# The q projection of two chunks as one Strassen pair, moved behind wo of the first chunk

## The chip, the cores and the metric

The kernel runs on one core of one Trainium2 chip. The metric is the device time of one execution in microseconds (us), lower is better. A core has a matrix engine (TensorE), a vector engine (VectorE), a scalar engine (ScalarE), GpSimd, and SyncE, which only issues transfers. Each engine works through its own instructions in order and waits on semaphores for the others. Sixteen DMA engines move data between device memory and the on-chip memory. In the profile the engines are called PE, DVE, ACT, POOL and SP.

## The reference, cut to what matters

One transformer layer on 2048 tokens of width 1024: layer norm, q, k and v of 32 heads of 32, attention of each position to itself and seven earlier ones at a stride of two, the output projection wo, a residual, then a second norm and a gated feed-forward part (FFN).

```python
qkv = (x @ wqkv) -> q, k, v                       # 32 heads of 32
idx = pos[:, None] - arange(8)[None, :] * 2        # 8 positions each
logits = einsum("bhsd,bhswd->bhsw", q, k[idx]) * 32 ** -0.5
o = einsum("bhsw,bhswd->bhsd", softmax(logits), v[idx])
h = x + o @ wo
g, u = layernorm(h) @ w_gate, layernorm(h) @ w_up
return h + (g * u) @ w_down
```

Inputs and outputs are bfloat16.

## The kernel before

The tokens are split into four chunks of 512. TensorE makes q, k and v of a chunk in 24 groups of 8 matmuls (6 weight blocks of 4 groups: blocks 0 and 1 are q, 2 and 3 are k, 4 and 5 are v). ScalarE copies each group out of PSUM (the memory into which TensorE writes; this kernel uses it as eight banks of 512 columns), SyncE stores it to device memory, GpSimd loads the whole of a chunk back in another layout for VectorE. VectorE does the attention. Its output takes the same way: one store of 1 MB (`od`), four reloads of a quarter each (`oT`), and then wo on TensorE.

```python
def attention(c):                                  # VectorE, about 84 us a chunk
    ...                                            # 4 x products q * k, sums: lg
    nc.scalar.activation(lg[:], lg[:], ACTF.Exp, scale=float(DH) ** -0.5)
    ...                                            # sums, 1/sum, 4 x products with v: oD
    nc.gpsimd.dma_start(od[c].rearrange("c g d s -> (c g) d s"), oD[:])
    oT = att.tile([128, KO, 4, SUB], BF, tag="oT", name=f"oT{c}")
    for cp in range(4):
        nc.gpsimd.dma_start(oT[:, :, cp, :], od[c][cp].rearrange("(hg hl) d s -> (hl d) hg s", hl=4))
    ...

def abs_down():                                    # ScalarE: sums of |w_down| for a later stage
    ring = wpool.tile([128, KO, 512], BF, tag="w", name="w_ring")
    ...
    for p in range(2):
        load(p)                                    # a load that ScalarE issues itself
    yield "later", 12.0
    for p in range(7):
        scale_d.add(p, rows_of(p), rows_of(p))
        ...
```

A generator such as `attention` or `abs_down` is background work. After each group of TensorE a scheduler, which runs when the kernel is built, takes the next steps of it. So the order within VectorE and ScalarE is fixed at build time, by a model of time.

The main order, cut:

```python
qkv(0, range(1, 4))
load_qk(0)                                         # q and k of chunk 0 back, for attention 0
...
bg.add(norm1[3].sums(), bg.now + 18.0)             # norm of chunk 3 on ScalarE
start_attention(0)
sums = abs_down()
bg.add(sums, bg.now + 25.0, first=True)
qkv(1, range(4))
qkv(0, range(4, 6))
load_v(0)
bg.add(norm1[3].rows(), bg.now, first=True)
qkv(1, range(4, 6))
start_attention(1)
...
qkv(2, range(6))
...
qkv(3, range(4), last=True)                        # q and k of chunk 3; frees weights
bg.finish(atts[0])
...
nxt = wo_ln2(0)                                    # wo of chunk 0 and its norm on VectorE
qkv(3, range(4, 6), last=True)                     # v of chunk 3: fills TensorE meanwhile
...                                                # then the FFN of chunk 0
```

Of the kernel before, what the change touches and what calls it, by code (L numbers as in the profile page):

```python
# [18 lines left out]
D = 1024  # L19
# [59 lines left out]
def kernel(  # L79
# [45 lines left out]
    bg = Background()  # L125

# [132 lines left out]
    class NormOnScalar(Norm1):  # L259
# [16 lines left out]
        def devs(self):  # L276
            nc.scalar.activation(self.nm, self.s, ACTF.Copy, scale=-1.0 / D)
            for t in range(4):
                nc.scalar.activation(self.junk[:], self.xs[t][:], ACTF.Square, bias=self.nm[:, t:t + 1],
                                     accum_out=self.ss[:, t:t + 1])  # L280
                yield "later", self.pace
            nc.scalar.activation(self.rs4[:], self.ss, ACTF.Ln, bias=eps[:], scale=1.0 / D)
# [17 lines left out]
        def rows(self):  # L300
            for t in range(4):
                self.row(t)
                self.transpose(t)
                yield "later", self.pace

# [33 lines left out]

    qkv_in = {}  # L340

    def evac_qkv(c, m, ps):
        sg = t1k.tile([128, HB + TC], BF, tag="t1k", name=f"sg{c}_{m}")
        nc.scalar.copy(sg[:, HB:HB + TC], ps[:])  # L344
# [5 lines left out]
        if m < 8:  # L350
            nc.sync.dma_start(qd[c][:, 4 * hg:4 * hg + 4, :, :].rearrange("c g d s -> (g d) c s"),
                              sg[:, HB:HB + TC].rearrange("p (c s) -> p c s", c=4))
# [81 lines left out]
    def qkv(c, blocks, last=False):  # L434
        for b in blocks:
            for j in range(4):
                ps = psum.tile([128, TC], F32, tag="mm", name=f"ps{c}_{b}_{j}")
                mm_group(ps, wts["qkv", b], j, lnTs[c])
# [9 lines left out]
    def load_qk(c):  # L448
        qD = att.tile([128, DH, SUB], BF, tag="qD", name=f"qD{c}")
        kD = att.tile([128, DH, SUB + HB], BF, tag="kD", name=f"kD{c}")  # L450
        nc.gpsimd.dma_start(qD[:], qd[c].rearrange("c g d s -> (c g) d s"))
# [98 lines left out]
    class Norm2(NormOnScalar):  # L550
# [11 lines left out]
        def finish(self):  # L562
            yield from self.devs()
# [5 lines left out]
    def wo_norm(c):  # L569
# [4 lines left out]
        for t in range(4):  # L574
            for hf in range(2):
# [6 lines left out]
                if hf == 0 and t > 0:  # L582
                    n.sum(t - 1)
                bg.step(GROUP_US)
        n.sum(3)
        retire(2)
        return n

    def wo_ln2(c, at={}):
        lnT = lnTp.tile([128, KO, TC], BF, tag="lnT", name=f"lnT2_{c}")  # L590
        hs = hss[c]
        mv4, rs4 = ln_tiles(f"2_{c}")

        def norm(t):
            ln = normalize(hs[t], mv4, rs4, t)
            nc.sync.dma_start_transpose(lnT[:, :, bass.ts(t, 128)], ln[:])

        for t in range(4):
            for hf in range(2):
                ps = psum.tile([128, 512], F32, tag="mm", name=f"wo{c}_{hf}_{t}")  # L600
                for kk in range(KO):
                    nc.tensor.matmul(ps[:], lhsT=oTs[c][:, kk, t, :], rhs=wts["wo", c, hf][:, kk, :],
                                     start=(kk == 0), stop=(kk == KO - 1))
                nc.vector.tensor_tensor(hs[t][:, bass.ts(hf, 512)], ps[:], hs[t][:, bass.ts(hf, 512)], ALU.add)
                if hf == 1:
                    stats(hs[t], mv4, t)
                    rstd_of(mv4, rs4, t, t + 1)
                    bg.spend(1.5)
                elif t > 0:
                    norm(t - 1)  # L610
                    bg.spend(0.55)
                bg.spend(0.7)
                if 2 * t + hf in at:
                    at[2 * t + hf]()
                bg.step(GROUP_US)
        norm(3)
        retire(2)
        for t in range(4):
            rows = hsd[c][:, t, :]
            nc.sync.dma_start(rows, hs[t][:, D - rows.shape[-1]:D])  # L620
        return lnT, hs



    ones = const.tile([128, 128], BF)
    nc.vector.memset(ones[:], 1.0)

    class Scale:
        def __init__(self, name, n):
# [724 lines left out]
```

## Time and profile before

| | before |
|---|---|
| time, median of the first 3 runs | 771.18 us (770.24 to 771.34) |
| profiled span, mean granted TensorE clock | 768.7 us, 1.000 |
| TensorE busy | 99% |
| VectorE busy | 79% |
| wo of chunk 0 starts | 163.45 us |
| FFN starts | 191.07 us |

TensorE is busy nearly all of the time and has almost no waits, so the span is close to the number of 512-column matmuls times 0.216 us plus the start. The prediction below shows the lines for that. Three more views matter for what follows. First the timeline of GpSimd (start, length, engine, line, operation, tiles, count, and in brackets the idle time before it and what ended it), with the k load of attention 0 (`kD`) and the store of its output (`od`):

```profile
44.12 0.54 POOL L452 DMA_DIRECT2D kD<-kd  x1 [12.56 <-DMA kd<-sg]
...
136.85 0.54 POOL L536 DMA_DIRECT2D od<-oD  x1 [47.11 <-DVE oD L534]
```

Second the transfers issued between 125 and 165 us (tiles, issuing queue, count, size of each, and the median time from issue to landing in us):

```profile
od<-oD POOLq DMA_DIRECT2D x1, 1024.0 KB, 4.2
```

The store of 1 MB took 4.2 us. It was not quite alone: SyncE issued four loads of 256 KB from 138.10 us on. But both wo weight loads (1 MB each) were issued after it had landed, from 145.50 us on. Third the timeline of ScalarE where it issues the first two loads of the down weights:

```profile
66.72 1.16 ACTq L671 DMA_DIRECT2D w_ring<-in_B_w_down_dram  x2
```

That held ScalarE's queue for 1.16 us.

### The profile page before, as it was taken

The page shows a single profiled execution, that of the slowest core. Times are in us where ns is not written, and L with a number is a line of the kernel's source. Part 1 is how long each engine was busy: PE and PEld are TensorE (multiplying, and loading weights), DVE is VectorE, ACT ScalarE, POOL GpSimd, SP SyncE. Part 2 cuts the span into 40 slices and gives each one's busy share as a digit, 9 for nine tenths or more (in the row PEclk, how much of TensorE's full clock was granted, in tenths as well). Part 3 has the DMA queues.
Part 4 walks back from the last instruction along what each step waited for, and adds up shares of the span by engine and source line. Part 5 has one row for each costly group of instructions (what it writes and reads, how often), then busy time and mean ns, then how long its engine had stood idle before and what let it go on. Part 6 is the DMA issues. An engine that isn't in the chain of part 4 may idle for free.

```text
span 768.7 us, 10302 instructions
## 1 busy us (share of the span) xinstructions
PE 762.8 (99%) x3663; PEld 350.7 (46%) x3663; DVE 606.0 (79%) x718; ACT 513.1 (67%) x979; POOL 142.5 (19%) x152
## 2 busy tenths in 40 slices
PE   8999999999999999999999999999999999999998
PEld 5444444444444444444444444444444444444444
DVE  5639999999999999999998997975454444568863
ACT  4648966423687398778899986736777677788240
POOL 0000000200002000020000001018778677600000
PEclk9999999999999999999999999999999999999999
DMA  8999796999966699579559448674342423730001
GB/s 268 272 257 260 207 269 153 279 305 283 301 219 216 210 299 294 172 246 326 194 186 300 139 155 279 126 198 107 80 110 55 110 74 91 257 126 29 0 29 55
DMA packets 190915, 144.85 MB, mean 188 GB/s; under 512 B 81808, under 2 KB 181136, under 8 KB 188688
## 3 DMA queue, kind: packets, MB, share of 16 engines
q1 hardware_dynamic: 180416, 116.94, 54.2%
q0 software_dynamic: 3584, 22.02, 8.4%
q10 hardware_dynamic: 6864, 5.24, 2.5%
q8 instruction: 28, 0.46, 0.2%
q14 instruction: 23, 0.19, 0.1%
HBM read 110.10 MB, written 27.26 MB: 179 GB/s over the span
## 4 chain that ended last, share of the span: by engine, by line
PE 97%; DVE 2%; DMA 1%; issue 0%; ACTq 0%; DVEq 0%
PE ps L431 21%; PE dx L944 6%; PE pz L826 6%; PE pwu L431 6%; PE pu L431 6%; PE py L826 6%; PE pwg L431 6%; PE pg L431 6%; PE px L826 6%; PE wo L998 4%; PE pv L826 3%; PE ez L944 3%; PE ey L944 3%; PE ex L944 3%; PE dy L944 3%; PE wo L578 2%
## 5 line engine op out<-in xcount | busy, mean ns | idle before, releaser
L431 PE MATMUL ps<-lnT,w_qkv 128*128 128x512 bf16 x736 | 159.5, 379 | 0.0
L431 PEld LDWEIGHTS <-w_qkv 128*128 128x128 bf16 x736 | 71.9, 98 | 86.1 <-issue 0.2
L344 ACT CAST sg<-ps 128x512 bf16<-128x512 f32 x96 | 55.2, 586 | 46.9 <-PE ps L431 41.6
L477 DVE TENSOR_TENSOR prod<-qD,kD 128x4096 bf16<-128x4096 bf16 x32 | 72.2, 2284 | 12.8 <-DMA kD<-kd 12.8
L523 DVE TENSOR_TENSOR pv<-vD,at 128x4096 bf16<-128x4096 bf16 x32 | 72.4, 2285 | 0.2
L826 PEld LDWEIGHTS <-sw 128*128 128x128 f16 x448 | 43.8, 98 | 52.9 <-issue 0.2
L431 PEld LDWEIGHTS <-w_wu 128*128 128x128 bf16 x448 | 43.8, 98 | 52.9
L431 PEld LDWEIGHTS <-w_wg 128*128 128x128 bf16 x448 | 43.8, 98 | 52.9
L826 PE MATMUL px<-lnT,ws 128*128 128x512 bf16 x224 | 55.2, 379 | 0.0
L536 POOL DMA_DIRECT2D od<-oD x4 | 2.2, 544 | 275.6 <-DVE oD L534 275.6
L431 PE MATMUL pg<-lnT,w_wg 128*128 128x512 bf16 x224 | 52.9, 379 | 0.0
L431 PE MATMUL pu<-lnT,w_wu 128*128 128x512 bf16 x224 | 52.9, 379 | 0.0
L431 PE MATMUL pwu<-lnT,w_wu 128*128 128x512 bf16 x224 | 52.9, 379 | 0.0
L431 PE MATMUL pwg<-lnT,w_wg 128*128 128x512 bf16 x224 | 52.9, 379 | 0.0
L826 PEld LDWEIGHTS <-ws 128*128 128x128 f16 x336 | 32.9, 98 | 39.6
L807 POOL TENSOR_TENSOR sw<-ws 128x512 f16<-128x512 f16 x26 | 30.0, 1155 | 82.4 <-PE pv L826 49.1
L944 PEld LDWEIGHTS <-gs 128*128 128x128 f16 (+1 forms) x280 | 27.4, 98 | 33.0
L479 DVE TENSOR_TENSOR prod<-prod 128x4096 bf16<-128x4096 bf16 x16 | 36.6, 2288 | 0.4
L843 ACT COPY py<-px 128x512 f32<-128x512 f32 x28 | 16.0, 570 | 27.7 <-PE px L826 27.7
L808 POOL TENSOR_TENSOR sw<-sw,ws 128x512 f16<-128x512 f16 x26 | 30.0, 1154 | 2.0
L810 POOL TENSOR_TENSOR sw<-ws,sw 128x512 f16<-128x512 f16 x26 | 30.3, 1167 | 0.0
L809 POOL TENSOR_TENSOR sw<-ws 128x512 f16<-128x512 f16 x26 | 30.1, 1156 | 0.0
(334 smaller groups left out, 1472.9 us busy)
## 6 DMA issues: line engine op xcount, KB each, us to landing
w_wg<-in_B_w_gate_dram SPq DMA_DIRECT2D x14, 1024.0 KB, 6.9
w_wu<-in_B_w_up_dram SPq DMA_DIRECT2D x14, 1024.0 KB, 6.3
w_pair<-in_B_w_gate_dram SPq DMA_DIRECT2D x14, 512.0 KB, 4.0
w_pair<-in_B_w_up_dram SPq DMA_DIRECT2D x14, 512.0 KB, 5.3
w_wo<-in_A_wo_dram SPq DMA_DIRECT2D x6, 1024.0 KB, 7.6
w_qkv<-in_A_wqkv_dram SPq DMA_DIRECT2D x5, 1024.0 KB, 11.5
kd<-sg SPq DMA_DIRECT2D x32, 144.0 KB, 4.4
kD<-kd POOLq DMA_DIRECT2D x4, 1152.0 KB, 8.6
```

The lines of the kernel that those rows point to most:

```text
L344: nc.scalar.copy(sg[:, HB:HB + TC], ps[:])
L431: nc.tensor.matmul(ps[:], lhsT=wt[:, ko, bass.ts(j, 128)], rhs=rhs[:, ko, :], start=(ko == 0), stop=(ko == KO - 1))
L477: nc.vector.tensor_tensor(prod[:, j], qD[:], kD[:, :, o:o + SUB], ALU.mult)
L479: nc.vector.tensor_tensor(prod[:, :, 0:16], prod[:, :, 0:16], prod[:, :, 16:32], ALU.add)
L523: nc.vector.tensor_tensor(pv[:, j], vD[:, :, o:o + SUB], at[:, w, None, :].to_broadcast((128, DH, SUB)), ALU.mult)
L807: eng.tensor_tensor(sw[:, i, 0], a21, a22, ALU.add)
L808: eng.tensor_tensor(sw[:, i, 1], sw[:, i, 0], a11, ALU.subtract)
L809: eng.tensor_tensor(sw[:, i, 2], a11, a21, ALU.subtract)
L810: eng.tensor_tensor(sw[:, i, 3], a12, sw[:, i, 1], ALU.subtract)
L826: nc.tensor.matmul(ps[:], lhsT=lhs[:, ko, :], rhs=rhs[:, ko, :], start=(fresh and ko == 0), stop=(ko == 3), skip_group_check=not fresh)
L944: nc.tensor.matmul(ps[:, bass.ds(lo, n)], lhsT=lhs[k][:, bass.ts(q, 128)], rhs=rhs[k][:, bass.ds(lo, n)], start=(fresh and k == 0), stop=( ...
L998: nc.tensor.matmul(ps[:], lhsT=oTs[c][:, kk, t, :], rhs=wts["wo", 2, hf][:, kk, :], start=(kk == 0), stop=(kk == KO - 1))
```

## The change

Strassen's scheme computes a 2 x 2 block product with 7 block products instead of 8. The change applies it to q of chunks 2 and 3 together (the two column blocks are the two chunks), with the halves of the contraction as the other dimension. It needs sums and differences of weight blocks and of activation rows in float16, so the q weights are first scaled by a power of two, which comes from the sum of their absolute values. That saves 16 matmuls. The pair also serves as filler: it stands behind wo of chunk 0, where TensorE computed v of chunk 3 before. Alongside, the first q load waits until chunk 1's transposes have landed, the norm of chunk 0 moves from VectorE to ScalarE, and the background work of ScalarE starts a little earlier.

The diff, cut to its core:

```diff
+    def add(self, k, src, junk):                  # class Scale, only moved up
+        nc.scalar.activation(junk, src, ACTF.Abs, accum_out=self.l1[:, k:k + 1])
 ...
-    def load_qk(c):
+    def load_qk(c, after=None):
 ...
+        if after is not None:
+            nc.gpsimd.tensor_copy(qD[:, 0, 0:1], after)
 ...
-    qkv(0, range(1, 4))
-    load_qk(0)
+    qkv(0, [1], at={(1, k): (lambda k=k: q_abs(k)) for k in range(4)})
+    qkv(0, [2], at={(2, 2): scale_q.rows})
+    qkv(0, [3], at={(3, 2): scale_q.total, (3, 3): q_convert})
+    load_qk(0, after=lnTs[1][:, 0, TC - 1:TC])
+    start_attention(0)
+    qkv(1, [2])
 ...
-    bg.add(norm1[3].sums(), bg.now + 18.0)
+    bg.add(norm1[3].both(), bg.now + 16.0, first=True)
     sums = abs_down()
-    bg.add(sums, bg.now + 25.0, first=True)
-    qkv(1, range(4))
+    bg.add(sums, bg.now + 18.0, first=True)
+    qkv(1, [3, 0, 1])
 ...
-    qkv(2, range(6))
+    qkv(2, range(2, 6))
 ...
-    qkv(3, range(4), last=True)
+    qkv(3, range(2, 6), last=True)
     bg.finish(atts[0])
 ...
-    nxt = wo_ln2(0)
-    qkv(3, range(4, 6), last=True)
+    rows_q = q_row_sums()                         # 12 + 1 sums of activation rows, VectorE
+    bg.add(rows_q, bg.now, first=True)
+    norm2 = [wo_norm(0, devs=False)]
+    bg.finish(rows_q)
 ...
+    for m0 in (0, 2):
+        q_pair(m0, room_q)                        # 112 matmuls instead of 128
```

## The prediction

> **What bounds the kernel now.** I began with the page: busy shares, the 40 slices, the chain that ended last.
>
> ```profile
> span 768.7 us, 10302 instructions
> PE 762.8 (99%) x3663; PEld 350.7 (46%) x3663; DVE 606.0 (79%) x718; ACT 513.1 (67%) x979; POOL 142.5 (19%) x152
> PE   8999999999999999999999999999999999999998
> DVE  5639999999999999999998997975454444568863
> PE 97%; DVE 2%; DMA 1%; issue 0%; ACTq 0%; DVEq 0%
> ```
>
> TensorE is busy from about 17 us to the end and is 97% of the chain, so removing matmuls pays directly. But VectorE has next to no air between slices 4 and 22 (about 77 to 420 us). A shorter TensorE stretch there pays only as far as VectorE's results are there in time. So I read next the timeline of TensorE where the change acts (columns: start, length, engine, line, operation, tiles, count).
>
> ```profile
> 27.04 136.57 PE L431 MATMUL ps<-lnT,w_qkv 128*128 128x512 bf16 x632
> 163.45 13.98 PE L602 MATMUL wo<-w_wo,oT 128*128 128x512 bf16 x64
> 177.26 13.98 PE L431 MATMUL ps<-lnT,w_qkv 128*128 128x512 bf16 x64
> 191.07 1.89 PE L431 MATMUL pg<-lnT,w_wg 128*128 128x512 bf16 x8
> 253.23 13.98 PE L578 MATMUL wo<-w_wo,oT 128*128 128x512 bf16 x64
> ```
>
> No idle time stands in any of these lines. 64 matmuls take 177.26 - 163.45 = 13.81 us, which is 0.216 us each, and a group of 8 takes 1.727 us. (The 379 ns that the groups view gives for one is latency.) Then VectorE, and GpSimd's issues, for the two attention chunks whose outputs TensorE needs at 163.45 and at 253.23:
>
> ```profile
> 52.34 4.49 DVE L477 TENSOR_TENSOR prod<-qD,kD 128x4096 bf16<-128x4096 bf16 x2 [12.77 <-DMA kD<-kd]
> 134.26 2.29 DVE L534 TENSOR_TENSOR oD<-oD,pv 128x4096 bf16<-128x4096 bf16 x1
> 172.30 1.28 DVE L604 TENSOR_TENSOR h<-wo,h 128x512 bf16<-128x512 f32 x2
> 141.35 3.55 POOL L539 DMA_DIRECT2D oT<-od x4 [3.96 <-DMA od<-oD]
> 244.34 3.54 POOL L539 DMA_DIRECT2D oT<-od x4 [6.39 <-DMA od<-oD]
> ```
>
> Attention 0 waits for its k load until 52.34, then runs without a gap of note to 136.55. Its output passes through memory: the first quarter of oT was issued at 141.35 and took 6.6 us to land, so it is there at 147.95, 15.5 us before use. For chunk 1 it lands at 244.34 + 3.7 = 248.05, 5.2 us before use. The first addition of wo in VectorE (172.30) is some 7 us behind TensorE's first finished group (163.45 + 1.9): VectorE is still in attention 1, and the eight PSUM banks hide that.
>
> Last, ScalarE near the start, and the price of one absolute sum of a 128x2048 block:
>
> ```profile
> 29.75 2.77 ACTq L231 DMA_TRANSPOSE lnT<-ln  x2
> 33.00 0.57 ACT L344 CAST sg<-ps 128x512 bf16<-128x512 f32 x1
> 80.57 1.91 ACT L635 ACTIVATE w_ring<-w_ring 128x2048 bf16<-128x2048 bf16 x1
> ```
>
> The second of the two transposes for chunk 1 is issued at 31.2 and takes 7.7 us, so it lands at 38.9. TensorE starts chunk 1 at about 39.1 (12 groups and two small transposes after 17.51). That edge has 0.2 us of slack.
>
> **What the Trainium skill says.** "TensorE: Matmul & The Clock Gate", section Back-to-back issue gap, gives N/2.4 + 2.5 ns for an isolated matmul, which is 216 ns at N = 512, and about 131 ns sustained. The trace has 216 ns in a stream of weight loads and matmuls; I count with that. "VectorE: DVE Perf Modes", section The perf-mode tier table, puts a 16-bit tensor_tensor of 2048 elements at 1224 ns; the trace agrees (1.22 to 1.23 us for 128x2048). "DMA: Bandwidth & Descriptors", section Issuing engines are not separate DMA queues, says that transfers started by any engine share the same 16 DMA engines. The trace fits: the first of those transposes took 3.4 us, the one that ran beside the 1 MB q load (issued 30.85) took 7.7. This is what the added wait on the first q load is for.
>
> **The change part by part.**
>
> Removed from TensorE: q of chunks 2 and 3 is 2 chunks x 8 blocks x 8 = 128 matmuls. The Strassen pair is 4 block pairs x 7 products x 4 = 112. So 16 fewer at 0.216 = 3.45 us. Added: one 64-column matmul for the scale, about 0.05 us (estimate, from 0.216 us at 512 columns). Net 3.40 us, the ceiling: 771.18 - 3.40 = 767.8. float16 weights against bfloat16 activations change nothing: that mix already runs at the same 379 ns latency in the gate and up stage.
>
> Moved: the 16 groups of q now come after wo of chunk 0, where 8 v groups stood after it before. So 8 groups fewer come before wo, which starts 8 x 1.727 = 13.8 us earlier, at 149.6. Attention 0's first quarter lands at 147.95: the slack falls from 15.5 to 1.7 us.
>
> ScalarE, added near the start: four absolute sums of 1.91 = 7.6 us between 19 and 31 us. Idle there was about 3 us. I put them into its order of work by hand: the rstd of chunk 1's last rows slips from 26.97 to about 31, the two transposes from 29.75 to about 33.4, and the last k eviction of chunk 0 from 40.2 to about 42.6. The second transpose, issued at 34.8 and now without the q load beside it, should take 4 to 5 us and land at 39 to 40: a TensorE wait of 0 to 1 us. The k load of attention 0 starts some 2 us later (46 for 44.12) and again takes about 8. So attention 0 starts later by a shift that I set at 1.5 us, between 0 and 2.5.
>
> VectorE, added: conversion of two weight blocks 2 x 1.28, sixteen sums of 128x512 at 0.34 (14 such took 4.78 us late in the trace) = 5.5, and scale arithmetic about 1: 9 us. These fit the 12.77 us in which it waited for the k load, so they are free. In the stretch from wo of chunk 0 on: row sums 12 x 0.34 + 1.22 = 5.3, eight Strassen outputs at 0.66 = 5.3. Removed there: statistics and normalisation of chunk 0, 8.2 us (between 172.30 and 185.62, less eight additions of 0.65), which ScalarE takes over. Net +2.4 us on VectorE before attention 1 ends.
>
> ScalarE in that stretch: per row tile 1.06 + 0.24 + 1.15 = 2.45 us of sum and deviation. I counted the order of issue from the kernel's own credits. About 21 us of attention 1 stand ahead of the first wo addition, so that runs at 136.6 + 1.5 + 21.4 = 159.5. The second is done at 160.8, and three tiles' sums keep ScalarE until about 168.2. Only then does it copy the first product into the second Strassen bank (0.57). TensorE wants that bank at 149.6 + 13.8 + 3 x 0.864 = 166.0. That is a wait of some 2 to 3 us; waits before it count towards it, not on top. The row sums, about 170 for the last, ask for about the same.
>
> At wo of chunk 1: attention 1 ends at 237.1 + 2.4 + 1.5, less about 1 us of idle time absorbed, so 240. Its first quarter lands 11 us later, at 251. TensorE would come at 253.23 - 3.40 = 249.8 without stalls and at about 252 with them: no further wait, or a few tenths.
>
> Sum: -3.40 + about 2.4 of new waits = -1.0, which gives 770.2. The placing of the sums and the added wait look tuned against just such stalls, and my hand order tends to stack delays that partly overlap. I take about half a microsecond back: 769.6.
>
> **The rivals.**
>
> (1) The whole gain shows, 767.8. For it: TensorE had no idle time at all before, and VectorE's new work falls into a hole of 12.77 us. Against: slack of 0.2 us at the transposes and 1.7 us at oT.
>
> (2) VectorE becomes the bound between 50 and 253 us. Then a later start of attention 0 (2.5 us or more) reaches oT at 149.6, the row sums and wo of chunk 1, and the saving is eaten: 771 to 773. For it: the VectorE row of nines, net +2.4 us there. Against: all these waits overlap, so the largest counts, not their sum.
>
> (3) The late attention stages suffer: attention 2 now starts only after the pair, and attention 3 falls one operation (2.3 us) behind by 395 us. For it: oT of chunk 3, issued at 463.45, lands at 467.3 for a use at 473.06. Against: 5.8 us of slack there, and VectorE waits of 1.5 and 0.4 us near 420 that absorb most of it. Worth 0 to 1 us.
>
> **Range and chances.** The best end is 767.8 less run-to-run scatter of half a microsecond; the bad end is rival 2 with some of rival 3. Range 767.4 to 772.4. Two per cent is 15.4 us: a gain of that size is impossible with 3.4 us removed; a loss of it would need a hang-up that I cannot see. Faster 0.01, same 0.97, slower 0.02.
>
> **What would show it.** TensorE has 3648 instructions (3663 - 16 + 1). Wo of chunk 0 starts near 150 to 151. A TensorE wait of 0 to 1 us shows before chunk 1's first group (39 to 41 us), and one of 1 to 3 us in the first Strassen products (165 to 170), ended by ScalarE's copy or by the row sums. Attention 0's first product starts at 52 to 55. No TensorE idle time of note follows 255 us. The prediction is wrong if TensorE shows no idle time in either place (then 768), or if attention 0 starts after 55 (then 771 and over).

## The result, and the profile after

The changed kernel gives correct results and took 780.51 us (778.02 to 781.51, 4 runs), beside 770.91 us for the kernel before in the same rounds. The ratio is 1.012, with a 95% interval of 1.0095 to 1.0146. Here and below a ratio is the mean time of one kernel's fast runs over the mean of the other's of the same rounds, so it is not quite the ratio of the medians quoted. Within 2% that counts as the same, which was the class predicted; the time is outside the predicted range, on the slow side. All profiles compared are of fast runs.

The page of the kernel after (span; busy time, share and count of each engine; clock in tenths over 40 slices; chain that ended last):

```profile
span 778.2 us, 10280 instructions
...
PE 759.9 (98%) x3592; PEld 349.5 (45%) x3648; DVE 621.7 (80%) x748; ACT 538.5 (69%) x1017; POOL 143.0 (18%) x153
...
PEclk9999999989999999999999999999999999999999
...
PE 49%; DVE 26%; ACT 13%; DMA 6%; issue 5%; SPq 0%; ACTq 0%; DVEq 0%
```

The weight loads are 3648, as predicted. (The matmul records are fewer because a few per cent are missing from such a trace.) TensorE was 97% of the chain before and is 49% now: the chain runs for 45% of the span through VectorE, ScalarE and transfers. In the ninth slice, 156 to 175 us, the clock falls by a step. The timeline of TensorE shows where:

```profile
157.59 15.90 PE L646 MATMUL wo<-w_wo,oT 128*128 128x512 bf16 x63 [6.85 <-DMA oT<-od]
...
181.22 1.02 PE L934 MATMUL qz<-lnT,qs 128*128 128x512 f16 x4 [0.84 <-ACT qz L974]
...
261.06 13.99 PE L646 MATMUL wo<-w_wo,oT 128*128 128x512 bf16 x63
...
508.68 12.25 PE L1067 MATMUL ez<-t,a22r 128*128 128x512 f16 x56 [1.20 <-DVE hsr L787]
```

TensorE came to wo of chunk 0 at 150.73 us and waited 6.85 us for oT. Then the same 64 matmuls took 15.90 us instead of 13.98. The stretches around it (start and end, length, then busy us and count on PE, PEld, DVE, ACT, POOL, then clock, DMA share and GB/s):

```profile
154.00:158.00 4.00, 0.41 (x2) 0.14 (x3) 3.96 (x3) 0.00 (x0) 0.24 (x1) 0.58 1.09 283
158.00:161.00 3.00, 3.00 (x9) 1.07 (x8) 2.93 (x3) 0.00 (x0) 0.00 (x0) 0.50 1.10 253
161.00:164.00 3.00, 3.00 (x14) 1.35 (x13) 1.60 (x3) 0.12 (x1) 0.00 (x0) 0.92 0.97 387
```

The granted clock was 0.50 from 158 to 161 us, after the idle time. The Trainium skill, "TensorE: Matmul & The Clock Gate", section HAM oscillation — how this bites in real kernels, says to keep TensorE from idling for more than about 3.4 us, as the clock is halved then. This trace agrees: TensorE stopped at 150.74 us, and the granted clock means of 0.58, 0.50 and 0.92 put the fall to half at about 154.6 us (an estimate from these three), some 3.9 us later. It was full again at about 161.5 us, so wo ran at half clock for about 3.9 us and lost 1.92. The prediction had no such term.

So the 9.5 us by which the span grew can be added up from TensorE's timeline:

| term | us |
|---|---|
| 16 matmuls fewer, one small one more | -3.40 |
| late by 150.73 us (149.6 expected; 0.54 and 0.34 us of it are waits for a free PSUM bank near 100 and 111 us) | +1.1 |
| wait for oT | +6.85 |
| half clock | +1.92 |
| the pair takes 25.48 us instead of 112 x 0.216 = 24.2 (0.84 of it the wait at 181 us) | +1.3 |
| after 261 us (1.2 of it the wait at 508 us) | +1.7 |
| sum | +9.5 |

Why oT was late is seen on VectorE and GpSimd. VectorE:

```profile
57.24 4.50 DVE L531 TENSOR_TENSOR prod<-qD,kD 128x4096 bf16<-128x4096 bf16 x2 [6.83 <-DMA kD<-kd]
...
103.32 0.69 DVE L556 TENSOR_TENSOR trs<-lg 128x512 f32<-128x512 f32 x1 [1.16 <-ACT lg L553]
```

GpSimd:

```profile
48.16 0.54 POOL L506 DMA_DIRECT2D kD<-kd  x1 [8.96 <-DMA kd<-sg]
...
141.73 0.54 POOL L590 DMA_DIRECT2D od<-oD  x1 [45.98 <-DVE oD L588]
...
150.14 3.55 POOL L593 DMA_DIRECT2D oT<-od  x4 [7.87 <-ACT sg L397]
```

SyncE's issue of the second wo weight load, and the store among the transfers issued between 125 and 165 us:

```profile
139.50 0.92 SPq L172 DMA_DIRECT2D w_wo<-in_A_wo_dram  x1
```

```profile
od<-oD POOLq DMA_DIRECT2D x1, 1024.0 KB, 7.9
```

Attention 0 starts 4.9 us later than before (57.24 for 52.34), because its k load is issued 4.0 us later (48.16 for 44.12) and takes 0.9 us longer. Its output is issued 4.9 us later (141.73 for 136.85). The store then takes 7.9 us instead of 4.2, so that the reloads are issued 8.4 us after it instead of 4.5, and the first of them lands after 7.4 us instead of 6.6. Together, 4.9 + 3.9 + 0.8, that is 9.6 us on a slack of 1.7. ScalarE shows one thing more, in the stretch before attention 0's exponential:

```profile
66.06 5.05 ACTq L674 DMA_DIRECT2D w_ring<-in_B_w_down_dram  x2
71.16 1.06 ACT L277 ACTIVATE njunk<-x 128x1024 bf16<-128x1024 bf16 x1 [5.51 <-DMA kd<-sg]
```

The same two load issues as before now hold ScalarE for 5.05 us (they take 0.37 and 0.45 us themselves; the rest lies between them). From there on it has no idle time of note until it reaches the exponential at 102.23 us.

### The profile page after: what moved, and what is told of

Read it like the earlier page. It is cut to its first block, busy times and chain, and to the rows that moved or that the text cites. A ratio compares the mean times of both kernels' runs of the same rounds, so it can differ in the third digit from the quotient of the medians.

```text
span 778.2 us, 10280 instructions
## 1 busy us (share of the span) xinstructions
PE 759.9 (98%) x3592; PEld 349.5 (45%) x3648; DVE 621.7 (80%) x748; ACT 538.5 (69%) x1017; POOL 143.0 (18%) x153
## 4 chain that ended last, share of the span: by engine, by line
PE 49%; DVE 26%; ACT 13%; DMA 6%; issue 5%; SPq 0%; ACTq 0%; DVEq 0%
PE ps L480 11%; PE dx L1067 6%; PE pz L829 6%; PE py L829 6%; PE px L829 6%; DVE pv L577 5%; DVE prod L531 4%; PE pv L829 3%; PE dy L1067 3%; PE wo L646 2%; DVE pv L586 2%; DVE prod L533 2%; DVE oD L588 2%; DMA b21r<-in_B_w_down_dram 2%; PE ez L1067 2%
## 5 line engine op out<-in xcount | busy, mean ns | idle before, releaser
L480 PE MATMUL ps<-lnT,w_qkv 128*128 128x512 bf16 x595 | 131.4, 379 | 1.6 <-ACT halo L399 0.9
L480 PEld LDWEIGHTS <-w_qkv 128*128 128x128 bf16 (+1 forms) x608 | 59.2, 98 | 72.2 <-issue 1.4
L394 ACT CAST sg<-ps 128x512 bf16<-128x512 f32 x72 | 41.8, 586 | 19.7 <-PE ps L480 13.7
L829 PE MATMUL px<-lnT,ws 128*128 128x512 bf16 x212 | 53.1, 379 | 0.6
L810 POOL TENSOR_TENSOR sw<-ws 128x512 f16<-128x512 f16 x26 | 30.0, 1155 | 79.6 <-ACT pz L854 48.0
L646 PE MATMUL wo<-w_wo,oT 128*128 128x512 bf16 x126 | 29.8, 397 | 7.0 <-DMA oT<-od 6.8
```

Of the source, the lines that this page charges most:

```text
L394: nc.scalar.copy(sg[:, HB:HB + TC], ps[:])
L480: nc.tensor.matmul(ps[:], lhsT=wt[:, ko, bass.ts(j, 128)], rhs=rhs[:, ko, :], start=(ko == 0), stop=(ko == KO - 1))
L646: nc.tensor.matmul(ps[:], lhsT=oTs[c][:, kk, t, :], rhs=wts["wo", c, hf][:, kk, :], start=(kk == 0), stop=(kk == KO - 1))
L810: eng.tensor_tensor(sw[:, i, 0], a21, a22, ALU.add)
L829: nc.tensor.matmul(ps[:], lhsT=lhs[:, ko, :], rhs=rhs[:, ko, :], start=(fresh and ko == 0), stop=(ko == 3), skip_group_check=not fresh)
```

## The experiments

My theory after this comparison: nearly all of the loss is the late oT and its half clock. Rival explanations were that VectorE and ScalarE have become the bound and would take the time in another place, and that the Strassen work itself, not the order, costs it. Then came the question why oT is late. The runs are told in that order.

**wo of chunk 0 from other data.** The wait is taken away by letting wo read an operand that is there. The result is wrong on purpose.

```diff
-                    nc.tensor.matmul(ps[:], lhsT=oTs[c][:, kk, t, :], ...
+                    lhs = oTs[c][:, kk, t, :] if c else lnTs[2][:, kk, bass.ts(t, 128)]
+                    nc.tensor.matmul(ps[:], lhsT=lhs, ...
```

> The changed kernel, but the output projection (wo) of chunk 0 reads the normalised rows of chunk 2, which are there long before, instead of attention 0's output. Wrong result on purpose. Theory (late input: the loss is TensorE's wait for attention 0's output, 6.85 us, and the 1.9 us of half clock that follow it): 780.5 - 6.85 - 1.9 = 771.8, range 771 to 773.5, no idle at wo of chunk 0. Rival (VectorE is the bound, the wait only moves on to wo of chunk 1 or to the Strassen sums): 776 or more, with 4 to 6 us of idle time at wo of chunk 1 or in the pair.

It took 775.07 us (774.5 to 776.0), ratio 1.0057. On TensorE's timeline wo now runs at full speed, but the pair waits:

```profile
150.62 13.98 PE L647 MATMUL wo<-w_wo,lnT 128*128 128x512 bf16 x63
...
171.39 1.87 PE L935 MATMUL qy<-qt,qs 128*128 128x512 f16 x4 [2.29 <-ACT qy L967]
```

5.4 us of the 8.8 came back. The rest moved to the waits in the first products that the prediction had placed there: 2.29 us for ScalarE's copy, and 1.5 us for the row sums. So the oT wait hid them. This lies between theory and rival: oT is the largest part, but while attention 0 ends late, the next waits stand right behind it.

**Thirty useless matmuls before wo.** They keep TensorE busy while it would idle.

```diff
+    idle = psum.tile([128, TC], F32, tag="mm", name="idle_ps")
+    for _ in range(30):
+        nc.tensor.matmul(idle[:], lhsT=ones[:], rhs=lnTs[2][:, 0, :], start=True, stop=True)
```

> The changed kernel with 30 matmuls of no use (6.5 us) ahead of wo of chunk 0, so that TensorE is busy while it waits for attention 0's output. Right result. If the half clock for some 3.4 us after the idle time costs 1.9 us (64 matmuls in 15.9 us for 13.98): 778.3 to 779.2, wo again in 14.0 us, idle before it under 1 us. If the slow start of wo comes from anything else: 780 to 781.

It took 777.98 us (776.97 to 778.39), ratio 1.0089, correct, with the clock at 1.000. That is 2.5 us less than the changed kernel, somewhat more than the 1.92 us read from the timeline; wo also started 0.6 us earlier there (157.00 for 157.59), because attention 0's output was issued 0.4 us earlier, so about 1.9 us are the clock's. The half clock is a cost of its own, beside the wait that causes it.

**The order without the Strassen work.** All moves of the change, but q of chunks 2 and 3 as plain matmuls: no sums, no scale, no pair.

```diff
-    qkv(0, [1], at={(1, k): (lambda k=k: q_abs(k)) for k in range(4)})
-    qkv(0, [2], at={(2, 2): scale_q.rows})
-    qkv(0, [3], at={(3, 2): scale_q.total, (3, 3): q_convert})
+    qkv(0, [1, 2, 3])
 ...
-    for m0 in (0, 2):
-        q_pair(m0, room_q)
+    for c in (2, 3):
+        qkv(c, [0, 1])
```

> The changed kernel's order of blocks (q of chunks 2 and 3 after wo of chunk 0, the wait of the first q load), but q of chunks 2 and 3 as 128 plain matmuls: no absolute sums, no conversion, no weight or row sums. Right result. If the order alone brings the loss (wo 13.8 us earlier, beside the weight loads): TensorE waits 2 to 5 us at wo of chunk 0 and the time is 773.5 to 778. If the order is harmless and only the added work of the Strassen form hurts: 770.5 to 771.5, no wait.

It took 779.17 us (778.79 to 779.88), ratio 1.011, correct, with 7.06 us of waiting for oT. So the new order alone, with nothing saved, costs 8.3 us. Attention 0 started on time here, at 52.49 us, and still ended late, because VectorE then waited 5.22 us for the exponential.

**A fixed scale.** The absolute sums and the scale's arithmetic are left out; the scale is the constant 1/8, which is right for these inputs only.

```diff
-    qkv(0, [1], at={(1, k): (lambda k=k: q_abs(k)) for k in range(4)})
-    qkv(0, [2], at={(2, 2): scale_q.rows})
-    qkv(0, [3], at={(3, 2): scale_q.total, (3, 3): q_convert})
+    scale_q.s, scale_q.inv = fixed[:, 0:1], fixed[:, 1:2]        # 0.125 and 8.0
+    qkv(0, [1, 2])
+    qkv(0, [3], at={(3, 3): q_convert})
```

> The changed kernel without the four absolute sums on ScalarE and the scale arithmetic: the scale is a constant (1/8 and 8, a power of two that fits this input). Right result. If the sums' 7.6 us on ScalarE are what makes attention 0 late: its first product starts at 53 to 54 instead of 57.2, the wait at wo of chunk 0 falls from 6.9 to 2 to 4 us, 775 to 777. If the crowded memory traffic at 141 to 158 us is what counts, the wait stays above 5 us and the time above 778.

It took 778.21 us (777.63 to 778.76), ratio 1.0096, correct. VectorE's timeline shows why so little was gained:

```profile
102.14 0.69 DVE L556 TENSOR_TENSOR trs<-lg 128x512 f32<-128x512 f32 x1 [4.97 <-ACT lg L553]
```

The k load was on time and attention 0 started at 52.26 us, but VectorE waited 4.97 us for the exponential. Its output was issued at 140.55 us, 1.2 us earlier only, and the wait for oT stayed 6.81 us.

**The first q load without its wait.**

```diff
-    load_qk(0, after=lnTs[1][:, 0, TC - 1:TC])
+    load_qk(0)
```

> The changed kernel with the first q load not waiting for chunk 1's transposes. Right result. Theory: attention 0's start is set by its k load, which waits for the k stores, so freeing the q load does not make it start earlier (57 us, plus or minus 1) and the wait at wo of chunk 0 stays at 6 to 7.5 us; what the added wait bought is chunk 1's transposes, which would now land later and stop TensorE for 0 to 3 us at 39 to 43 us. Time 779.5 to 783. Rival (the added wait is what delays attention 0): 775 to 778, first product at 53 to 54.

It took 782.76 us (781.95 to 787.92), ratio 1.0167, correct. TensorE now waited 2.3 us near 41 us for chunk 1, and the k load was no earlier (issued at 48.96 us). The transposes of chunk 1 landed 6.9 to 7.4 us after their issue, for 3.3 in the changed kernel. So this part of the change works as meant and is worth about 2.3 us; it isn't what delays attention 0.

**What the store of attention 0 competes with.** Four runs take away traffic beside it. In the first, no weight is loaded between the first wo weight and the arrival of oT.

```diff
+                if held.get("after") is not None:
+                    nc.gpsimd.tensor_copy(wt[:, 0, 0:1], held["after"])
 ...
-    qkv(3, range(2, 6), last=True)
+    qkv(3, [2], last=True)
+    held["on"] = True
+    qkv(3, range(3, 6), last=True)
     bg.finish(atts[0])
+    held["on"], held["after"] = False, oTs[0][:, 0, 3, 0:1]
+    pump()
```

> The changed kernel, with the gate and up weight loads that were issued at 145 to 162 us held back until attention 0's output has landed. Right result. If their 3 MB beside the output's way through memory cost what the traces suggest (7.9 us for the store and 7.4 for the first reload, against 4.2 and 6.6 before): the wait at wo falls by 3 to 4.5 us and the time to 775 to 777.5. If the traffic does not matter: 780 to 781.

As a timing it is spoilt: I had held the second wo weight too, TensorE waited 8.84 us for it, and the time was 783.68 us (782.54 to 785.28), ratio 1.0164. As a measurement of the store it is of use. In the second run both wo weights load as usual, and only the gate and up weights are held:

```diff
-                if held.get("after") is not None:
+                if held.get("after") is not None and key[0] != "wo":
 ...
-    qkv(3, [2], last=True)
-    held["on"] = True
-    qkv(3, range(3, 6), last=True)
+    qkv(3, [2, 3], last=True)
+    held["on"] = True
+    qkv(3, [4, 5], last=True)
```

> As e5_weights_held, mended: there the second wo weight was held too, and TensorE waited 8.8 us for it. Now only gate and up weights are held until attention 0's output is there. In e5 the store took 6.0 us and the first reload 5.2 (7.9 and 7.4 in the changed kernel) and the wait for the output was 2.4 us. So the wait falls from 6.9 to 2 to 4 us and the time to 774.5 to 777.5. If the saving in e5 came from the missing wo load: above 779.

778.71 us (775.98 to 779.73), ratio 1.0088, correct; the wait for oT stayed 6.94 us. That hides a gain: attention 0's output was issued 1.7 us later here (143.47 us), and from that issue to wo it took 14.1 us instead of 15.9. The third run leaves the weights alone and has the v rows of chunk 3 stored 27 us earlier, beside chunk 2's and from their data (wrong on purpose):

```diff
+        if c == 3 and m >= 16:
+            return
         dst = (kd, vd)[m // 8 - 1][c]
 ...
+        if c == 2 and m >= 16:
+            nc.sync.dma_start(vd[3][:, 4 * hg:4 * hg + 4, :, :].rearrange("c g d s -> (g d) c s"), win)
```

> The changed kernel, except that chunk 3's v rows are not stored while they are computed (137 to 151 us); the same number of bytes is stored into their place 27 us earlier, beside chunk 2's v stores, from chunk 2's data. The outputs of chunk 3 are wrong on purpose; the work of every engine is otherwise the same. Theory (the small-packet v stores are what stretches attention 0's output store from 4.2 to 7.9 us): that store lands in 5.5 us or less, TensorE's wait for oT at wo of chunk 0 falls from 6.85 to under 4.8 us, the clock dip gets shorter, and the time is 775.5 to 778.0. Rival (the second wo weight load, issued two microseconds before the store, is what it competes with): the store still takes over 6.8 us and the time is within 1.2 us of the changed kernel's 780.5.

779.81 us (779.78 to 780.5), ratio 1.0122, the store at 7.8 us: the rival's numbers. The fourth does both, and was meant to leave only the second wo weight load beside the store:

> As e10_v_stores_elsewhere, and the gate and up weight loads also wait until attention 0's output has been reloaded, so that beside the output store only the second wo weight load is left. Chunk 3 wrong on purpose. Theory (v stores): store and first quarter reload together take under 10 us instead of 15.8, the wait for oT is under 3.5 us, and the time is 773.5 to 777.0. Rival (second wo weight load): the store still takes over 6.0 us and the wait for oT stays above 5 us.

776.16 us (774.65 to 777.26), ratio 1.0077. The store took 7.7 us, again the rival's number; the wait for oT fell to 3.76 us, about as the theory had it, but through the reloads. The store in the runs with everything held, with gate and up held, and with both kinds of traffic away, one fence each:

```profile
od<-oD POOLq DMA_DIRECT2D x1, 1024.0 KB, 5.7
```

```profile
od<-oD POOLq DMA_DIRECT2D x1, 1024.0 KB, 7.8
```

```profile
od<-oD POOLq DMA_DIRECT2D x1, 1024.0 KB, 7.7
```

The first two runs differ, as edits, in the second wo weight load, and the store in 2.1 us. The fourth run is less clean than it was meant to be: taking traffic away moved the loads, so that the first wo load, issued at 137.16 us and under way for 6.7 us, was the one ahead of the store (141.29 us), and the second came 1.45 us behind it. What all 18 profiles have in common is this. In 13 of them a 1 MB wo load was issued 0.9 to 4.3 us ahead of the store and was still under way, and the store took 7.0 to 9.8 us. In the other five it took 4.2 to 5.8 us: in three no wo load was under way (4.2, 4.6 and 5.7), in two one came 1.2 to 1.8 us behind the store (5.0 and 5.8). These are single profiles that differ in other traffic too, so it is no clean test. But it agrees with the first two runs: of the 3.7 us that the store lost, a weight load ahead of it is about two. The rest, from 4.2 to 5.7 us, goes with what is left in the first run, the stores of chunk 3's k and v among it; that was not taken apart further. The reloads behave otherwise: the first quarter came 3.9 us after its issue where gate and up loads and v stores were both away, 5.7 us with the gate and up loads alone away, and 7.3 us with the v stores alone away.

**Other places for the pair.** If TensorE reaches wo too early, the pair could stand before it. In the first such run the whole pair does, the row sums run on GpSimd to spare VectorE, and v of chunk 3 goes behind wo again.

```diff
-            nc.vector.tensor_tensor(t1[k], b12[:, k, :], b11[:, k, :], ALU.subtract)
+            nc.gpsimd.tensor_tensor(t1[k], b12[:, k, :], b11[:, k, :], ALU.subtract)
 ...
-    qkv(3, range(2, 6), last=True)
+    qkv(3, [2, 3], last=True)
 ...
+    for m0 in (0, 2):
+        q_pair(m0, room_q)
+    norm2 = [wo_norm(0, devs=False)]
 ...
+    qkv(3, [4, 5], last=True)
```

> Another order that keeps the 16 matmuls saved: the Strassen pair before wo of chunk 0 (row sums on GpSimd, which is idle then), v of chunk 3 after wo as in the kernel before. Wo of chunk 0 then starts at about 160 us where attention 0's output is there at about 155 to 158. Right result. If the late output is the whole loss of the change: no wait at wo, 768 to 771. If VectorE is the bound, its eight Strassen outputs stand behind attention's work, the PSUM banks run out in the pair (waits of 2 to 6 us) and the time is 772 to 777.

808.31 us (806.22 to 812.42), ratio 1.049, correct, a clear failure. GpSimd's timeline:

```profile
112.33 12.00 POOL L918 TENSOR_TENSOR qt<-lnT,lnT 128x512 f16<-128x512 bf16 x4 [16.92 <-ACT sg L397]
```

VectorE's products of 128x4096 beside these sums took 3.13 us instead of 2.29. A row sum took 3.0 us; GpSimd's sums of 128x512 later in the kernel take 1.16, but those read float16 and these bfloat16, so that is no like comparison. The Trainium skill, "SBUF — State Buffer", section SBUF: two separate sides, says that these two engines share a pair of memory ports that one of them locks for an instruction while the other blocks; the trace agrees in that VectorE became slower; that GpSimd did too is likely, not shown. TensorE waited 11.4 us for the sums and then 17.1 us for the norm of chunk 0, whose transposes SyncE issued between stores from 209.5 to 223.0 us (ScalarE had finished the rows at 214.0 us).

The second run puts only half of the pair before wo and keeps the row sums on VectorE.

```diff
-    bg.add(rows_q, bg.now, first=True)
-    norm2 = [wo_norm(0, devs=False)]
-    bg.finish(rows_q)
+    for us in rows_q:
+        bg.spend(us)
     room_q = wpool.tile([128, 4, TC], F32, tag="w", name="room_q")
+    q_pair(0, room_q)
+    norm2 = [wo_norm(0, devs=False)]
 ...
-    for m0 in (0, 2):
-        q_pair(m0, room_q)
+    q_pair(2, room_q)
```

> The changed kernel with the first half of the pair (output blocks 0 and 1) moved ahead of wo of chunk 0; the row sums stand on VectorE directly behind attention 0, and the second half of the pair stays behind wo as filler. Results correct. Theory (most of the loss is TensorE reaching wo of chunk 0 before its attention output is back from memory at about 157.5 us, plus the half clock after that idle time): wo now starts at about 163, shows no wait for oT of note, the FFN starts at 189 to 192 us instead of 198.8, and the time is 770.5 to 774.0, still above the ceiling of 767.8 for the 1.1 us of PSUM waits near 105 us and the 1.2 us wait near 500 us, which this edit leaves. Rival (the loss only changes its place: the row sums, the ScalarE copies or the norm of chunk 0, which now has 12 us of TensorE work to hide behind instead of 24, take over): the FFN starts after 194 us and the time is 776 or more.

808.56 us (807.63 to 809.3), ratio 1.0487, correct. wo had no wait any more, but TensorE's timeline has two others:

```profile
161.78 0.61 PE L934 MATMUL qv<-qt,qs 128*128 128x512 f16 x1 [9.08 <-DVE qt L917]
...
220.19 3.18 PE L480 MATMUL pg<-lnT,w_wg 128*128 128x512 bf16 x8 [17.18 <-DMA lnT<-ln]
```

The row sums stood behind 20 us of attention 1 that VectorE had already been given. The norm of chunk 0 came late again. The rival was right: the loss changes its place, and the first of the two waits is for VectorE.

The third has, in addition, the norm rows of chunk 3 on ScalarE back where the kernel before has them.

```diff
-    bg.add(norm1[3].both(), bg.now + 16.0, first=True)
+    sums3 = norm1[3].sums()
+    bg.add(sums3, bg.now + 18.0)
 ...
     load_v(0)
+    bg.finish(sums3)
+    bg.add(norm1[3].rows(), bg.now, first=True)
```

> As e8_half_pair_first, and the norm rows of chunk 3 on ScalarE go back to where the kernel before has them, behind the v load of chunk 0, with their sums two microseconds later. Theory (attention 0's exponential is late at 102 us, and PSUM is freed late between 100 and 111 us, because the rows of chunk 3 stand ahead of it on ScalarE): VectorE's wait for the exponential falls from about 5 to under 3 us or attention 0 ends at least 1.5 us earlier than in e8, TensorE's waits between 95 and 115 us fall below 0.4 us, and the time is 0.7 to 1.5 us below e8. Rival (the ScalarE load that issues the down weights and waits for the queue holds it, not the rows): attention 0 ends within 0.7 us of e8's, and the time is within 0.6 us of it, or the transposes of chunk 3 come late for its v and k groups and it is slower.

812.22 us (811.28 to 814.52), ratio 1.0543, correct. VectorE's wait for the exponential grew to 5.28 us, from 1.12 in the run before it, instead of falling. ScalarE did the sums and rows just before the exponential now. The theory about these rows fell; the 5 us for which ScalarE is held while it issues loads were still there, at 65.5 us.

**Both causes of attention 0's late end.** That led to the decisive pair of runs. The first starts the down weights' sums 9 us later, so that ScalarE issues their loads at another time; the second does the same with the fixed scale.

```diff
-    bg.add(sums, bg.now + 18.0, first=True)
+    bg.add(sums, bg.now + 27.0, first=True)
```

> The changed kernel, with the absolute sums of the down weights (whose first two loads ScalarE issues at 66 us and is held by for 5 us) started 9 us later. Results correct. If k load and ScalarE hold stand in parallel: the hold is gone or under 2 us, VectorE's wait for the exponential falls from 1.16 us to 0, but attention 0 ends at 140 to 141 instead of 141.4, because VectorE's own chain from the late k load decides; the PSUM waits between 95 and 115 us shrink; time 779.0 to 780.5. If the hold alone decides: attention 0 ends before 138, wait for oT under 4 us, time under 777. If neither: attention 0's end and the time are unchanged within 0.5 us.

> As e3_fixed_scale (k load on time), and the absolute sums of the down weights 9 us later. If both causes stand in parallel: attention 0 starts at 52.3, VectorE's wait for the exponential falls from 4.97 to under 2 us, attention 0 ends at 136.3 to 138, its output is issued by 138.3, TensorE's wait for oT falls from 6.8 to between 2 and 4.5 us (the store still meets the second wo weight load), time 773.0 to 776.0. If something else on ScalarE holds the exponential: attention 0 still ends after 139.5, time 777 or more.

The first took 780.42 us (778.52 to 787.61), ratio 1.0146; the second 769.24 us (768.64 to 769.67), ratio 0.9982, interval 0.9965 to 0.9998. Both are correct. In the first, on ScalarE and then on GpSimd:

```profile
74.75 1.07 ACTq L674 DMA_DIRECT2D w_ring<-in_B_w_down_dram  x2
...
101.97 1.06 ACT L553 ACTIVATE lg<-lg 128x1024 f32<-128x1024 f32 x1 [5.63 <-DVE lg L551]
```

```profile
141.47 0.54 POOL L590 DMA_DIRECT2D od<-oD  x1 [47.31 <-DVE oD L588]
```

The hold is gone (and, by the same edit, one sum of 2.1 us has moved from before the exponential to behind it), and now ScalarE waits 5.63 us for VectorE, whose attention 0 still started at 57.02 us. Its output was issued at 141.47 us, as before this edit. One expectation missed: the waits for PSUM did not shrink but became one of 7.23 us at 110 us, in the place of the one for oT. ScalarE stood still there for 9.59 us from 106.4 to 116.0, around the issue of a later down-weight load, and in that time emptied no bank. The issue itself took 0.38 us, at 115.62; the profile puts the end of the standstill down to the down-weight load before it, issued at 91.52 us, which landed just then. So this run's time says little; its attention 0 is what counts. In the second run, one fence each for TensorE, VectorE, GpSimd and SyncE:

```profile
149.62 13.98 PE L646 MATMUL wo<-w_wo,oT 128*128 128x512 bf16 x63
```

```profile
52.34 4.50 DVE L531 TENSOR_TENSOR prod<-qD,kD 128x4096 bf16<-128x4096 bf16 x2 [5.63 <-DMA kD<-kd]
```

```profile
136.78 0.54 POOL L590 DMA_DIRECT2D od<-oD  x1 [46.48 <-DVE oD L588]
```

```profile
137.93 0.84 SPq L172 DMA_DIRECT2D w_wo<-in_A_wo_dram  x1
```

wo starts at 149.62 us, to the tenth where the prediction had put it. Attention 0 starts and ends where it did before. The store takes 5.0 us, and no wait for oT is left. So the late k load and the late ScalarE stand in parallel: in these runs attention 0's output is issued at 140 to 142 us with either of them present, and only taking away both brings the time back. How much of ScalarE's delay is the hold and how much the sum that moved with it is not separated: in the runs with the order alone and with the fixed scale the hold was 2.85 and 3.60 us, and VectorE still waited 5.22 and 4.97 us. The time came back further than I had expected (773 to 776): the store stood 1.15 us ahead of the second wo weight load this time (issued at 137.93 us), not behind it, and took 5.0 us instead of 7.9.

**A version with its scale computed.** The late k load should come from the four absolute sums on ScalarE. The next two runs keep the later down sums and put two, or all four, of them on VectorE.

```diff
+        if k in on_vector:                        # (0, 2), or all four
+            nc.vector.tensor_reduce(scale_q.l1[:, k:k + 1], wts["qkv", k // 2][:, bass.ts(k % 2, 4), :],
+                                    mybir.AxisListType.XY, ALU.add, apply_absolute_value=True)
+            return
```

Here `on_vector` stands for a list of engines written out in the kernel that ran.

> As e12_later_down_sums, with two of the four absolute sums of the q weights moved from ScalarE to VectorE. Results correct. Theory (the sums on ScalarE make the k load late, about 1 us for each): attention 0's first product starts at 53.5 to 55.5, its output is issued at 138 to 140, the wait for oT is 2 to 5 us, time 772.0 to 776.5. Rival (the scale's matmul and arithmetic do it): attention 0 starts after 56.5 and the time is over 778.

> As e12_later_down_sums, with all four absolute sums of the q weights on VectorE. Results correct. Theory: ScalarE is as early as in e13, attention 0's first product starts at 52 to 53, its output is issued by 137.5, TensorE waits under 0.6 us at wo of chunk 0, and the time is 768.8 to 770.5, at or just under the kernel before (770.4), unless the sums push VectorE's norm of chunk 1 so late that TensorE waits 1 to 3 us for chunk 1's transposes near 40 us; then 770.5 to 773. Rival (the scale's matmul and arithmetic make the k load late): attention 0 starts after 56 and the time is over 778.

With two sums on VectorE the kernel is correct and took 769.18 us (768.81 to 772.6, 6 runs), beside 770.68 us for the kernel before (11 runs): ratio 0.9989, interval 0.9973 to 1.0004. From its VectorE and TensorE timelines:

```profile
51.48 4.50 DVE L531 TENSOR_TENSOR prod<-qD,kD 128x4096 bf16<-128x4096 bf16 x2 [3.68 <-DMA kD<-kd]
```

```profile
149.47 13.98 PE L646 MATMUL wo<-w_wo,oT 128*128 128x512 bf16 x63
```

The k load was issued at 44.93 us, 0.8 us later than before and 3.2 us earlier than in the changed kernel, and attention 0 began even earlier than before. Two sums less gave back all of the delay, not half of it as I had expected: the last k eviction of chunk 0 ended at 40.45 us, as before (40.22), for 43.07 in the changed kernel. The rest of attention 0's earlier start is the load, which took 6.6 us instead of 9.1; why is not shown. With all four on VectorE the time was 784.65 us (781.6 to 787.72), ratio 1.0182. Each takes 2.28 us there and stands ahead of the norm of chunk 1. The k load was issued at 47.80 us and attention 0 began at 57.79 us, the rival's numbers, but not for its reason: the scale's matmul and arithmetic are in the run with two sums as well, and it was on time. TensorE also waited 5.77 us for a PSUM bank near 120 us, because ScalarE stood still for 10.63 us before it issued a down-weight load at 124.70 us. How long ScalarE stands at such an issue swings from run to run, and that makes these kernels touchy.

All runs at a glance (fast runs; the changed kernel is 780.51 us, ratio 1.012):

| what was run | us | ratio | wait for oT at wo of chunk 0, us |
|---|---|---|---|
| wo of chunk 0 from other data | 775.07 | 1.0057 | none |
| 30 useless matmuls | 777.98 | 1.0089 | none, filled |
| order only | 779.17 | 1.011 | 7.06 |
| fixed scale | 778.21 | 1.0096 | 6.81 |
| q load without wait | 782.76 | 1.0167 | 6.4 |
| all weights held | 783.68 | 1.0164 | 2.39 |
| gate and up held | 778.71 | 1.0088 | 6.94 |
| v stores elsewhere | 779.81 | 1.0122 | 7.23 |
| v stores and gate elsewhere | 776.16 | 1.0077 | 3.76 |
| pair before wo | 808.31 | 1.049 | not oT |
| half of the pair before wo | 808.56 | 1.0487 | none |
| the same, norm rows later | 812.22 | 1.0543 | none |
| later down sums | 780.42 | 1.0146 | none, 7.23 for PSUM |
| fixed scale and later down sums | 769.24 | 0.9982 | none |
| two sums on VectorE, later down sums | 769.18 | 0.9989 | none |
| four sums on VectorE, later down sums | 784.65 | 1.0182 | 2.29 |

## Why the prediction was right or wrong

**What held.** TensorE's work fell by 3.40 us as counted. The order on ScalarE near the start was placed well: the transposes were issued at 32.92 us (33.4 predicted), the last k evictions ran at 42 to 43 us (42.6), and TensorE did not wait at 39 to 41 us. VectorE's new work fitted its hole, with 6.83 us of idle time left. TensorE without delays would have reached wo at 149.6 us; the run with both causes removed reached it at 149.62. The waits of some 2 to 3 us in the first products were real: the run with other data for wo shows 2.29 us for ScalarE's copy. In the changed kernel they were hidden behind the larger wait. The third rival, 0 to 1 us in the late stages, did not come as told: oT of chunk 3 caused no wait. But 1.7 us were lost after 261 us all the same, 1.2 of them at 508 us in the FFN, ended by VectorE, so "No TensorE idle time of note follows 255 us" failed.

**The step that failed** is this one: "So attention 0 starts later by a shift that I set at 1.5 us, between 0 and 2.5", and with it the slack at oT, "Attention 0's first quarter lands at 147.95: the slack falls from 15.5 to 1.7 us". The k load was said to start some 2 us later and to take about 8 us again. It was issued 4.0 us later and took 9.1. The last k eviction on ScalarE ended 2.9 us later (43.07 for 40.22; 2.4 predicted), but a load starts when the stores of those blocks have landed, which added about 1.2 us more, and I had carried only the evictions through. The shift was 4.9 us, twice the upper end I gave. The run with two sums on VectorE, beside the one with later down sums only (57.02 us), shows the cause: with two absolute sums less on ScalarE the shift is gone (51.48 us).

**A second cause that the prediction had not seen** is ScalarE around 66 us. The diff moves the start of the down sums from 25 to 18 us in the scheduler's model, and hands out the norm of chunk 3 at another moment (its sums begin at 63.82 us, for 59.11 before). I read these as order only. In the run, ScalarE was held for 5.05 us while it issued the two loads, instead of 1.16, and the exponential of attention 0 came at 102 us whether or not VectorE was ready for it. The runs with a fixed scale and with the order alone show ScalarE's lateness in the open, and the decisive pair shows that it counts. The part of the hold alone is not separated, and why the issue is held is not shown. It was 1.07 us when it came 9 us later. In the holds of 5.05 and 9.59 us SyncE had just issued transposes, which would fit; so would, in the second, the landing of the load before it. No run tested either.

**The transfers were taken over unchanged** from the trace of before, 4.2 us for the store and 6.6 for the first reload. But the change moves the end of chunk 3's blocks, which free weight buffers, from after attention 0's output to just before it, and each freed buffer starts a 1 MB load. The store took 7.9 us, of which about two go with the weight load ahead of it, and the reload 7.4. Of the 9.6 us by which oT was late, about half is this.

**The clock** was a missing term: 1.92 us read from the timeline, and about as much by the run with useless matmuls (2.5 us, less 0.6 of an earlier start).

**The rule by which waits combine was right in kind.** "The largest counts" is what the other-data run shows. But the largest was one that I had put at zero. Rival 2 had the mechanism, a late attention 0 that reaches oT, and was sized at 771 to 773; with a shift of 4.9 us it should have had 3.2 us of waiting, and the crowded transfers and the clock made it 8.8. The prediction's own sign, "if attention 0 starts after 55 (then 771 and over)", fired at 57.24 us.

What is left after the repair: the version with two sums on VectorE gains 1.5 us on the kernel before by the medians (about 0.9 by the ratio of the means, as one of its runs took 772.6) out of the 3.4 counted, with 0.84 us lost in the pair at the same ScalarE copy as in the changed kernel, and about 1 us after wo of chunk 1 (2.3 us ahead there, 1.3 us ahead at the end). Its interval just touches no difference, so a gain of more than 0.3% is excluded and a small one is likely, not proved.

## What to carry to other kernels

When a change lets the bounding engine arrive earlier somewhere, the slack of everything it meets there shrinks by that much: recompute each link from issue to landing, with the transfers that will then be in flight, and do not take durations from a trace in which other transfers ran beside them. A delay can have two causes side by side, and taking either away alone then shows nothing; try both together before calling a cause wrong. An in-order engine that copies results out of PSUM should not be given extra work, or transfers to issue, ahead of the one result that another engine waits for.

## What the Trainium skill lacked or had wrong

- "TensorE: Matmul & The Clock Gate", section Back-to-back issue gap: about 131 ns sustained at 512 columns. No stretch of these traces comes near it; 64 matmuls with their weight loads take 13.81 us, 216 ns each, in both kernels.
- "TensorE: Matmul & The Clock Gate", section HAM oscillation — how this bites in real kernels: what it says was borne out, with 6.85 us idle followed by a granted clock of 0.50 and 1.92 us lost. What it does not say is that filling the wait with useless matmuls pays: about 1.9 us here (2.5 us less, 0.6 of it from an earlier start).
- "SBUF — State Buffer", section SBUF: two separate sides: it names the lock between VectorE and GpSimd, and quotes slowdowns without the operations they were taken on. Here a VectorE product of 128x4096 went from 2.29 to 3.13 us beside GpSimd sums of 128x512, which took 3.0 us each (GpSimd spans are rough; without VectorE's products this sum was not measured).
- "DMA: Bandwidth & Descriptors", section Issuing engines are not separate DMA queues: it says that transfers interleave and that the time to initiate one is usually small. Here a 1 MB store took 4.2 to 5.8 us with no weight load ahead of it and 7.0 to 9.8 us with one of 1 MB issued 0.9 to 4.3 us ahead and still under way, and ScalarE was held for 5.05 us at 66 us while it initiated two loads, against 1.07 us at 75 us, and stood still for 9.59 us before it initiated one at 116 us.
